# Attention's denominator and numerator in one two-bank PSUM tile, Newton's product in place, and the banks behind it dealt anew

## The chip, the cores and the metric

The kernel runs on one core of a Trainium2 chip. The metric is the device time of one execution in microseconds (us): here the median of three runs of the kernel before, beside one execution that the hardware profiler recorded. Engines are named as the profile names them: PE is TensorE (PEld its weight loads), DVE VectorE, ACT ScalarE, POOL GpSimd, SP SyncE, whose queue issues most DMAs.

## What is computed

Three stages follow one another. The first is a linear attention with random features, over 2 batches of 8 heads, 576 tokens each, head dimension 64 and 128 features. The second is a two-layer network with the activation h·tanh(softplus(h)), the third a mixture of 8 experts that sends each token to the expert with the largest gate logit. The change touches the end of the first, the gate of the third and the places where PSUM is shared out.

```python
def phi(x):                                   # x: q or k, scaled
    h = einsum('bhsd,md->bhsm', x, omega) - sum(x * x, -1) / 2
    return exp(h - max(h, -1)) / sqrt(m)
q_p, k_p = phi(q_s), phi(k_s)
kv  = einsum('bhsm,bhsd->bhmd', k_p, v)
num = einsum('bhsm,bhmd->bhsd', q_p, kv)
den = einsum('bhsm,bhm->bhs', q_p, sum(k_p, axis=2)) + 1e-06
x   = num / den                               # then the network, then:
logits = x @ w_gate; expert = argmax(logits)  # and the two expert matmuls per token
```

## The kernel before

**PSUM.** Every PSUM tile is one bank of 128 partitions by 512 float32 values, handed out by `bank(tag, name)` (L87): three buffers of the tag `pj`, two of `qt`, and one each of `b0`, `b1` and `b2`, eight banks in all. A matmul that writes a tag's only buffer has to wait until every reader of the previous tile of that tag is done.

**Attention** (L169 to L414) works on eight pairs of heads, p = 0 to 7. For each pair POOL, or ACT and DVE for the first ones, splits q and k into a rounded and a residual part (`split`, L213: `kqh`, `kql`); PE projects them on the features, four or five tiles t per pair (`proj`, L222, tile `pj`, three matmuls per product in `mm3`); DVE takes the negated maximum (`phi`, L240, tile `nm`), and DVE and ACT write the exponents (L245, L247, L250, tile `e`). PE turns q's part (`qtr`, L272, tile `qT`) and sums k's with v (`kvm`, L252, tile `kvp` in `b0`). Of the projections, (p, t) = (0, 3) and (1, 3) use `b1`, (1, 0) and (1, 4) use `b2`, all others `pj`.

Two pairs make a **unit** u = 0 to 3. When a unit's sums are complete, `den(u)` (L294) runs in three steps for two token halves c = 0, 1 of 288 tokens (GT) each: eight matmul passes per half into bank `b1` or `b2` (`heads`, L287); on ACT the logarithm and the exponential of its negative, a first estimate r of 1/den (L304, L305); on DVE a Newton step in two instructions, t = (den + eps)·r (L309), then r = (t − 2)·r (L311). Tile t lies in SBUF, so L311 reads two tensors from SBUF, while L309 reads one from PSUM and one from SBUF. `num(u, k)` (L313) runs twice per unit, k = 0 and 1, again with both halves in `b1` and `b2` (in the last unit k = 0 uses the two `qt` banks): eight passes per half on PE, then x = −num·r on DVE (L325), then the split of x into `xh` and `xl`, by POOL in two halves (L59, L63), in the last unit by ACT and DVE over both halves at once.

**Order.** The attention is written as beats (`beat`, L357): in beat t of pair i PE is given the projection (i, t) and whatever `pe` adds, DVE and ACT the work of phi, and the later steps of den and num come one beat after each other. den(u) starts in beat 0 of pair 2u + 3, num(u, 0) in its beat 2, num(u, 1) in beat 0 of pair 2u + 4. The order of instructions on each engine is then fixed when the kernel is built, by a planner that goes by the written order as priority, by estimated costs and by when buffers come free. From L431 on everything is in `manual_schedule`: each engine gets its instructions in the written order.

**Behind it** come the network's first matmul (`hmm`, L157, tile `h`), which starts in the gaps of the last unit, and its second (`ymm`, tile `py`). Column block 0 of `hmm` needs batch 0 alone, block 1 (L549) needs `xh` and `xl` of the last unit. The gate's logits lie in `b0`, `b1` and `b2` (`lg`, L434), are copied out (L800 to L802), turned per group of four token tiles into `b0`, `b1`, `b2` and summed over four parts on DVE, group by group (`route0`, L625, L633). The matmuls `py1` and `py2` of the experts use `b0`, `b1`, `b2` and one `qt` bank for output blocks d = 0 to 3 (L817, L834, L855). The branch from L894 on, for tokens left over, does not run with these inputs.

Of the kernel before, what the change touches and what calls it, by code (L numbers as in the profile page):

```python
# [9 lines left out]
F32 = mybir.dt.float32  # L10
# [5 lines left out]
AF = mybir.ActivationFunctionType  # L16
ALU = mybir.AluOpType
AX = mybir.AxisListType
# [15 lines left out]
def performer_mish_moe(  # L34
# [51 lines left out]

    def bank(tag, name):  # L87
        return psum.tile([128, 512], F32, name=name, tag=tag, bufs={"pj": 3, "qt": 2}.get(tag, 1))


    h3 = tc.alloc_tile_pool(name="h3", bufs=1)
# [77 lines left out]
    with ExitStack() as c2:  # L169
# [8 lines left out]

        wb = a1.tile([128, 512], BF16, name="wb")
        V.memset(wb, 0.0)  # L180
        wp = bank("b2", "wp")
        for _ in range(5):
            T.matmul(out=wp, lhsT=wb[:, 0:128], rhs=wb, start=True, stop=True)
        oms = a1.tile([128, 2 * M], F32, name="oms")
# [37 lines left out]
        def proj(p, t):  # L222
            d = st[p]

            first = {(0, 3): "b1", (1, 0): "b2", (1, 3): "b1", (1, 4): "b2"}
            d["p", t] = ps = bank(first.get((p, t), "pj"), "pj")
            for i in range(2):
                s = slice(256 * t + 128 * i, 256 * t + 128 * i + 128)
                if (p, t) == (0, 0):

                    T.matmul(out=ps[:, i * 256 : i * 256 + 256], lhsT=d["f"][:, s], rhs=oms, start=True, stop=True)
                    continue
                mm3(ps[:, i * 256 : i * 256 + 256], d["h"][:, s], d["l"][:, s], omh, oml, True, True)
# [60 lines left out]
        def den(u):  # L294

            d = st[u, "u"]
            d["r"] = r = a2.tile([128, SEQ], F32, name="r", tag="r", bufs=1)
            o = [bank(f"b{c + 1}", "den")[:, :GT] for c in range(2)]
            half = [r[:, c * GT : c * GT + GT] for c in range(2)]
            for c in range(2):  # L300
                heads(u, o[c], c, "z", slice(0, 32))
            yield
            for c in range(2):
                S.activation(out=half[c], in_=o[c], func=AF.Ln, bias=eps)  # L304
                S.activation(out=half[c], in_=half[c], func=AF.Exp, scale=-1.0)  # L305
            yield
            t = [a2.tile([128, GT], F32, name="t", tag="t") for c in range(2)]
            for c in range(2):
                V.scalar_tensor_tensor(out=t[c], in0=o[c], scalar=EPS, in1=half[c], op0=ALU.add, op1=ALU.mult)  # L309
            for c in range(2):  # L310
                V.scalar_tensor_tensor(out=half[c], in0=t[c], scalar=2.0, in1=half[c], op0=ALU.subtract, op1=ALU.mult)  # L311

        def num(u, k, last=False):  # L313

            b, e = divmod(2 * u, KT)
            r = st[u, "u"]["r"]
            x = a2.tile([128, SEQ], F32, name="xf", tag="xf")
            o = [bank("qt" if last and k == 0 else f"b{c + 1}", "num")[:, :GT] for c in range(2)]
            for c in range(2):
                heads(u, o[c], c, "kv", slice(k * 32, k * 32 + 32))  # L320
            yield
            yield
            for c in range(2):
                s = slice(c * GT, c * GT + GT)
                V.scalar_tensor_tensor(out=x[:, s], in0=o[c], scalar=-1.0, in1=r[:, s], op0=ALU.mult, op1=ALU.mult)  # L325
            c = slice(b * SEQ, b * SEQ + SEQ)
            if last:
                split_hi_lo(x, xh[:, e + k, c], xl[:, e + k, c], "act", "dve")
            else:
                for i in range(2):  # L330
                    s = slice(i * GT, i * GT + GT)
                    t = slice(b * SEQ + i * GT, b * SEQ + i * GT + GT)
                    split_hi_lo(x[:, s], xh[:, e + k, t], xl[:, e + k, t], "pool", "pool")

        eps = a1.tile([128, 1], F32, name="eps")
        V.memset(eps, EPS)
# [94 lines left out]
    with tc.manual_schedule():  # L431
        nc.sync.dma_start(out=wgf, in_=wgate)
        nc.sync.dma_start(out=capi, in_=cap.to_broadcast([TT, 1]))
        lg = [bank(f"b{c}", f"lg{c}")[:, 0:384] for c in range(3)]  # L434

        V.memset(onesb, 1.0)
        V.memset(tiny, 1e-30)
# [187 lines left out]
        def route0(lgs):  # L625
            sh = [TT, NTT, E]
            pv = small("pv", sh)
            for c in range(3):
                p = bank(f"b{c}", "rp")
                for i in range(4):  # L630
                    t = 4 * c + i
                    T.transpose(p[:TT, i * 128 : i * 128 + 128], lgs[:, t * TT : t * TT + TT], ident)
                V.tensor_reduce(  # L633
                    out=pv[:, 4 * c : 4 * c + 4, :],
                    in_=p[:TT, :].rearrange("p (t k e) -> p t e k", k=KT, e=32)[:, :, 0:E, :],
                    op=ALU.add,
                    axis=AX.X,
                )
                yield
            bc = lambda a: a[:, :, None].to_broadcast(sh)  # L640
            mx = small("mx", [TT, NTT])
            V.tensor_reduce(out=mx, in_=pv, op=ALU.max, axis=AX.X)
            V.tensor_tensor(out=pv, in0=pv, in1=bc(mx), op=ALU.subtract)
            ex = small("ex", sh)
            S.activation(out=ex, in_=pv, func=AF.Exp)

            cand = small("cand", sh)
            V.scalar_tensor_tensor(out=cand, in0=pv, scalar=0.0, in1=iota, op0=ALU.is_ge, op1=ALU.mult)
            idx = small("idx", [TT, NTT])
            V.tensor_reduce(out=idx, in_=cand, op=ALU.min, axis=AX.X)  # L650
# [194 lines left out]
        for f in range(8):  # L845
# [9 lines left out]
        py = [bank(t, "py2") for t in ("b0", "b1", "b2", "qt")]  # L855
# [38 lines left out]
    with tc.If(R["nrem"] > 0):  # L894
        with ExitStack() as c2:
# [3 lines left out]
            ob = q1.tile([TT, NTT, DM], F32, name="ob")  # L899
            V.memset(ob, 0.0)  # L900
            with tc.For_i(0, G, 1) as gi:
                ps = [bank(t, "pq") for t in ("pj", "b0", "b1", "b2")]
# [100 lines left out]
```

## Time and profile before

| | |
|---|---|
| three runs, median (lowest to highest) | 314.94 us (311.08 to 315.23) |
| profiled execution: its time, and its span | 315.25 us, span 313.4 us |
| mean granted clock of TensorE | 0.985 of full speed |
| busy share: PE, PEld, DVE, ACT, POOL | 95%, 87%, 67%, 62%, 31% |
| chain that ended last | PE 67%, DVE 16%, ACT 9%, issue 2%, DMA 2%, POOL 1% |

The span runs from the first to the last recorded instruction; the execution's time is 1.85 us longer. The attention fills the first 82 us or so, the network the stretch to about 222 us with the gate near 208 us, the two experts the rest. Busy shares are averages over these stages.

### The profile page before, as it was taken

How to read it: one execution, taken by the hardware profiler on the slowest of the kernel's cores; microseconds unless marked ns; L12 is line 12 of the kernel's file. 1: busy time of each engine (PE TensorE's matmuls, PEld its weight loads, DVE VectorE, ACT ScalarE, POOL GpSimd, SP SyncE). 2: the span in 40 equal slices, each digit the busy share in tenths (PEclk: the TensorE clock that was granted, in tenths of full speed). 3: DMA queues.
4: the chain of work that ended last, by engine and by line, in shares of the span. 5: the costliest groups of instructions: out<-in, count | busy, mean ns of one | idle time of the engine just before them, and what ended most of it. 6: DMA issues, size and time to landing. Idle time of an engine off the chain costs nothing.

```text
span 313.4 us, 6043 instructions
## 1 busy us (share of the span) xinstructions
PE 299.1 (95%) x2276; PEld 272.2 (87%) x2277; DVE 211.0 (67%) x390; ACT 193.9 (62%) x376; POOL 98.1 (31%) x127
## 2 busy tenths in 40 slices
PE   8999979999999999999999989999999999999991
PEld 5897848887899999879987987889899999999991
DVE  4757675894899887988498489999644572325320
ACT  3997754776127897876986997945535743426211
POOL 1889993306012111112010100159304450513300
PEclk9999995999999999999999999999999999999998
DMA  7857611112054727944233000000325535722011
GB/s 228 298 187 262 229 36 51 67 69 69 0 185 153 259 72 232 364 185 153 117 136 134 0 2 0 2 1 3 100 90 152 174 122 163 209 68 78 1 40 44
DMA packets 18066, 37.11 MB, mean 118 GB/s; under 512 B 1552, under 2 KB 7248, under 8 KB 18032
## 3 DMA queue, kind: packets, MB, share of 16 engines
q1 hardware_dynamic: 17888, 36.53, 35.3%
q8 instruction: 20, 0.33, 0.4%
q10 hardware_dynamic: 144, 0.13, 0.2%
q14 instruction: 14, 0.11, 0.1%
HBM read 33.12 MB, written 3.54 MB: 117 GB/s over the span
## 4 chain that ended last, share of the span: by engine, by line
PE 67%; DVE 16%; ACT 9%; issue 2%; DMA 2%; POOL 1%; SPq 0%; DVEq 0%; POOLq 0%; ACTq 0%
PE h L67 7%; PE h L68 6%; PE h L69 6%; PE py L68 5%; PE py L67 5%; PE py L69 5%; PE kvp L259 4%; PE pj L67 3%; PE num L292 3%; DVE g L483 3%; PE pj L69 3%; ACT em L481 3%; PE pj L68 2%; ACT L469 2%; PE qt L280 2%; PE ph L67 2%
## 5 line engine op out<-in xcount | busy, mean ns | idle before, releaser
L67 PE MATMUL h<-xh,wih 128*128 128x384 f32 x192 | 65.7, 342 | 1.6 <-DVE g L440 0.9
L68 PE MATMUL h<-xl,wih 128*128 128x384 f32 x192 | 64.4, 335 | 0.0
L69 PE MATMUL h<-xh,wil 128*128 128x384 f32 x192 | 64.3, 335 | 0.0
L63 POOL TENSOR_TENSOR wl<-wl,whi 128x512 fp32r<-128x512 f32 x27 | 37.3, 1392 | 84.4 <-ACT whi L57 67.2
L67 PEld LDWEIGHTS h<-xh,wih 128*128 128x128 f32 x192 | 36.0, 188 | 5.3 <-issue 3.5
L68 PE MATMUL py<-gh,whi 128*128 128x288 f32 x128 | 38.0, 297 | 0.8 <-DVE gh L63 0.8
L59 POOL TENSOR_SCALAR wih<-wif 128x512 fp32r<-128x512 f32 x13 | 11.7, 899 | 85.0 <-DVE wif L116 60.0
L67 PE MATMUL py<-gh,whi 128*128 128x288 f32 x128 | 38.3, 299 | 0.0
L69 PE MATMUL py<-gh,wl 128*128 128x288 f32 x128 | 37.7, 294 | 0.0
L68 PEld LDWEIGHTS h<-xl,wih 128*128 128x128 f32 x192 | 36.1, 188 | 0.5 <-issue 0.5
L240 DVE TENSOR_REDUCE nm<-pj 128x4 f32<-128x512 f32 x36 | 24.6, 689 | 17.1 <-PE pj L69 17.0
L69 PEld LDWEIGHTS h<-xh,wil 128*128 128x128 f32 x192 | 36.0, 188 | 0.0
L440 ACT COPY g<-h 128x384 f32<-128x384 f32 x36 | 16.0, 472 | 26.7 <-PE h L69 26.5
L63 DVE TENSOR_TENSOR gh<-g,gh 128x288 fp32r<-128x288 f32 x32 | 22.6, 715 | 12.4 <-ACT gh L57 12.3
L247 ACT ACTIVATE e<-pj,nm 128x128 f32<-128x128 f32 x72 | 22.8, 391 | 11.9 <-DVE nm L240 10.8
L483 DVE TENSOR_TENSOR g<-g,em 128x1152 f32<-128x1152 f32 x16 | 21.6, 1357 | 12.7 <-ACT em L481 12.6
L57 ACT CAST whi<-wl 128x512 fp32r<-128x512 f32 x43 | 25.4, 615 | 2.6 <-DMA wl<-w 1.4
L68 PEld LDWEIGHTS py<-gh,whi 128*128 128x128 f32 x128 | 24.1, 188 | 1.5 <-DVE gh L63 1.5
L63 POOL TENSOR_TENSOR kql<-kqf,kqh 128x256 fp32r<-128x256 f32 (+2 forms) x29 | 22.7, 801 | 7.6 <-ACT kqh L57 7.3
L67 PEld LDWEIGHTS py<-gh,whi 128*128 128x128 f32 x128 | 24.0, 188 | 0.9 <-issue 0.6
L69 PEld LDWEIGHTS py<-gh,wl 128*128 128x128 f32 x128 | 24.1, 188 | 0.0
L67 PE MATMUL pj<-omh,kqh 128*128 128x256 f32 x70 | 23.5, 336 | 0.5 <-ACT e L250 0.5
(151 smaller groups left out, 723.9 us busy)
## 6 DMA issues: line engine op xcount, KB each, us to landing
wi<-w_in SPq DMA_DIRECT2D x16, 512.0 KB, 3.6
wo<-w_out SPq DMA_DIRECT2D x16, 512.0 KB, 4.3
wl<-w SPq DMA_DIRECT2D x32, 256.0 KB, 2.8
out<-zero SPq DMA_DIRECT2D x1, 2304.0 KB, 11.9
kqf<-kq SPq DMA_DIRECT2D x3, 640.0 KB, 3.9
v<-va SPq DMA_DIRECT2D x4, 390.0 KB, 4.5
kqf<-kq SPq DMA_DIRECT2D x3, 512.0 KB, 4.0
v<-va SPq DMA_DIRECT2D x4, 260.0 KB, 5.2
```

Source lines behind the costliest of these rows:

```text
L57: S.copy(out=hi, in_=src)
L59: P.tensor_scalar(out=hi, in0=src, scalar1=1.0, scalar2=0.0, op0=ALU.mult, op1=ALU.add)
L63: e.tensor_tensor(out=lo, in0=src, in1=hi.bitcast(F32), op=ALU.subtract)
L67: T.matmul(out=o, lhsT=lh, rhs=rh, start=start, stop=False)
L68: T.matmul(out=o, lhsT=lh, rhs=rl, start=False, stop=False)
L69: T.matmul(out=o, lhsT=ll, rhs=rh, start=False, stop=stop)
L240: d["max"] = V.tensor_reduce(out=nm, in_=pv, op=ALU.max, axis=AX.X, negate=True)
L247: S.activation(out=e[:, j, :], in_=pv[:, j, :], func=AF.Exp, bias=nm[:, j : j + 1])
L259: T.matmul(out=K[:, c : c + 65], lhsT=e[t][:, h, :], rhs=v[:, (2 * t + h) * 65 : (2 * t + h + 1) * 65], start=(p % 2 == 0 and h == 0 and t ...
L292: T.matmul(out=o[32 * i : 32 * i + 32, :GT], lhsT=d[w][:, h, r, s], rhs=d["qT"][:, r, h, c * GT : c * GT + GT], start=True, stop=True, til ...
L440: (S.copy if 2 < j < 14 or (j < 3 and c == 2) else V.tensor_copy)(out=g(j, slice(c * 384, c * 384 + 384)), in_=ps)
L483: V.tensor_tensor(out=hv, in0=hv, in1=em.pop(j), op=ALU.mult)
```

## The change

A new function `twin` allocates one PSUM tile of two banks (tag `b12`), in place of the two tags `b1` and `b2`. den and num use it for both halves: each ACT and DVE step on them becomes one instruction over 2 × 288 values, t is written over den in PSUM, and x is split by POOL in one piece. The last unit's num(3, 0) keeps two `qt` banks and two DVE instructions. Projections (0, 3) and (1, 0) share one twin, (1, 3) and (1, 4) the next. In `route0` all twelve transposes come first, then two sums, one over group 0 and one over groups 1 and 2. The py tiles and the logits take `b0` and the twin's halves through `three`; in the second expert `qt` now holds block 2 and the twin's second half block 3.

```diff
+    def twin(name):
+        return psum.tile([128, 2, 512], F32, name=name, tag="b12", bufs=1)
+    def three(name):
+        t = twin(name)
+        return [bank("b0", name), t[:, 0, :], t[:, 1, :]]
...
-        wp = bank("b2", "wp")
+        wp = twin("wp")[:, 1, :]
...
-            first = {(0, 3): "b1", (1, 0): "b2", (1, 3): "b1", (1, 4): "b2"}
-            d["p", t] = ps = bank(first.get((p, t), "pj"), "pj")
+            if (p, t) in ((0, 3), (1, 3)):
+                st["twin"] = twin("pj")
+            first = {(0, 3): 0, (1, 0): 1, (1, 3): 0, (1, 4): 1}
+            d["p", t] = ps = st["twin"][:, first[p, t], :] if (p, t) in first else bank("pj", "pj")
...
-            d["r"] = r = a2.tile([128, SEQ], F32, name="r", tag="r", bufs=1)
-            o = [bank(f"b{c + 1}", "den")[:, :GT] for c in range(2)]
-            half = [r[:, c * GT : c * GT + GT] for c in range(2)]
+            d["r"] = a2.tile([128, SEQ], F32, name="r", tag="r", bufs=1)
+            r = d["r"].rearrange("p (c t) -> p c t", c=2)
+            o = twin("den")[:, :, :GT]
             for c in range(2):
-                heads(u, o[c], c, "z", slice(0, 32))
+                heads(u, o[:, c, :], c, "z", slice(0, 32))
             yield
-            for c in range(2):
-                S.activation(out=half[c], in_=o[c], func=AF.Ln, bias=eps)
-                S.activation(out=half[c], in_=half[c], func=AF.Exp, scale=-1.0)
+            S.activation(out=r, in_=o, func=AF.Ln, bias=eps)
+            S.activation(out=r, in_=r, func=AF.Exp, scale=-1.0)
             yield
-            t = [a2.tile([128, GT], F32, name="t", tag="t") for c in range(2)]
-            for c in range(2):
-                V.scalar_tensor_tensor(out=t[c], in0=o[c], scalar=EPS, in1=half[c], op0=ALU.add, op1=ALU.mult)
-            for c in range(2):
-                V.scalar_tensor_tensor(out=half[c], in0=t[c], scalar=2.0, in1=half[c], op0=ALU.subtract, op1=ALU.mult)
+            V.scalar_tensor_tensor(out=o, in0=o, scalar=EPS, in1=r, op0=ALU.add, op1=ALU.mult)
+            V.scalar_tensor_tensor(out=r, in0=o, scalar=2.0, in1=r, op0=ALU.subtract, op1=ALU.mult)
...
-            o = [bank("qt" if last and k == 0 else f"b{c + 1}", "num")[:, :GT] for c in range(2)]
+            if last and k == 0:
+                o = [bank("qt", "num")[:, :GT] for c in range(2)]
+            else:
+                t = twin("num")[:, :, :GT]
+                o = [t[:, c, :] for c in range(2)]
...
-            for c in range(2):
-                s = slice(c * GT, c * GT + GT)
-                V.scalar_tensor_tensor(out=x[:, s], in0=o[c], scalar=-1.0, in1=r[:, s], op0=ALU.mult, op1=ALU.mult)
+            if last and k == 0:
+                for c in range(2):
+                    V.scalar_tensor_tensor(out=x3[:, c, :], in0=o[c], scalar=-1.0, in1=r[:, c, :], op0=ALU.mult, op1=ALU.mult)
+            else:
+                V.scalar_tensor_tensor(out=x3, in0=t, scalar=-1.0, in1=r, op0=ALU.mult, op1=ALU.mult)
...
-            if last:
-                split_hi_lo(x, xh[:, e + k, c], xl[:, e + k, c], "act", "dve")
-            else:
-                for i in range(2):
...
-                    split_hi_lo(x[:, s], xh[:, e + k, t], xl[:, e + k, t], "pool", "pool")
+            split_hi_lo(x, xh[:, e + k, c], xl[:, e + k, c], *(("act", "dve") if last else ("pool", "pool")))
...
-        lg = [bank(f"b{c}", f"lg{c}")[:, 0:384] for c in range(3)]
+        lg = [x[:, 0:384] for x in three("lg")]
...
-            for c in range(3):
-                p = bank(f"b{c}", "rp")
+            r0, r12 = bank("b0", "rp"), twin("rp")
+            for c, p in enumerate((r0, r12[:, 0, :], r12[:, 1, :])):
                 for i in range(4):
...
-                V.tensor_reduce(
...
-                yield
+            for o, p in ((pv[:, 0:4, :], r0[:TT, :]), (pv[:, 4:12, :], r12[:TT, :, :].rearrange("p c f -> p (c f)"))):
+                V.tensor_reduce(out=o, in_=p.rearrange("p (t k e) -> p t e k", k=KT, e=32)[:, :, 0:E, :], op=ALU.add, axis=AX.X)
+            yield
...
-        ps1 = [bank(t, "py1") for t in ("b0", "b1", "b2", "qt")]
+        ps1 = [*three("py1"), bank("qt", "py1")]
...
-        py = [bank(t, "py2") for t in ("b0", "b1", "b2", "qt")]
+        py = three("py2")
+        py.insert(2, bank("qt", "py2"))
```

## Rows read from the trace of the kernel before

**Rows 1.** the page, busy time, share and instructions of TensorE and its weight loads

```profile
PE 299.1 (95%) x2276; PEld 272.2 (87%) x2277; DVE 211.0 (67%) x390; ACT 193.9 (62%) x376; POOL 98.1 (31%) x127
```

**Rows 2.** the chain that ended last, 40 to 56 us (start, us, what)

```profile
43.15 3.40 DVE r L311
46.55 0.38 DVE t L309
...
47.06 0.69 PE num L292 x8
```

**Rows 3.** who waited for whom (total us, times, longest)

```profile
PE num L292 <- DVE t L309: 2.1, 1, 2.1
```

**Rows 4.** by stretch: length; PE, PEld, DVE, ACT, POOL busy; PEclk; DMA share; GB/s

```profile
44.90:47.06 2.16, 0.03 (x1) 0.03 (x1) 2.16 (x3) 0.00 (x0) 2.08 (x4) 1.00 0.00 0
47.06:54.60 7.54, 7.54 (x43) 6.37 (x47) 4.04 (x9) 3.52 (x12) 2.53 (x5) 0.55 0.19 53
```

**Rows 5.** timeline of DVE, 20 to 50 us (start, us, engine, line, operation)

```profile
26.20 0.89 DVE L311 SCALAR_TENSOR_TENSOR r<-t,r 128x288 f32<-128x288 f32 x1
...
43.07 3.48 DVE L311 SCALAR_TENSOR_TENSOR r<-t,r 128x288 f32<-128x288 f32 x1
```

**Rows 6.** timeline of POOL, 18 to 50 us

```profile
44.45 1.42 POOL L63 TENSOR_TENSOR kql<-kqf,kqh 128x256 fp32r<-128x256 f32 x2
45.84 0.41 POOL L59 TENSOR_SCALAR kqh<-kqf 128x256 fp32r<-128x256 f32 x1
46.33 0.81 POOL L63 TENSOR_TENSOR kql<-kqf,kqh 128x256 fp32r<-128x256 f32 x1
```

**Rows 7.** DVE groups by line and shape (count, busy us, mean ns)

```profile
L311 DVE SCALAR_TENSOR_TENSOR r<-t,r 128x288 f32<-128x288 f32 x8 | 7.3, 920 | 0.0
...
L325 DVE SCALAR_TENSOR_TENSOR xf<-num,r 128x288 f32<-128x288 f32 x16 | 6.8, 451 | 1.1 <-PE num L292 1.0
...
L63 DVE TENSOR_TENSOR xl<-xf,xh 128x576 fp32r<-128x576 f32 x2 | 1.5, 760 | 0.0
```

**Rows 8.** ACT group of 576 elements, by line and shape

```profile
L57 ACT CAST xh<-xf 128x576 fp32r<-128x576 f32 x2 | 1.4, 678 | 2.1 <-DVE xf L325 2.1
```

**Rows 9.** timeline of all engines, 60 to 82 us (unit 2)

```profile
65.76 0.82 DVE L311 SCALAR_TENSOR_TENSOR r<-t,r 128x288 f32<-128x288 f32 x2
...
66.60 1.18 PE L292 MATMUL num<-qT,kv 128*32 128x288 f32 x16
...
70.11 0.43 POOL L59 TENSOR_SCALAR xh<-xf 128x288 fp32r<-128x288 f32 x1 [11.69 <-DVE xf L325]
```

**Rows 10.** the chain that ended last, 20 to 34 us (unit 0)

```profile
23.81 0.62 PE den L292 x8
...
26.90 0.62 PE num L292 x8
...
28.75 0.62 PE num L292 x8
...
31.93 1.11 PE num L292 x16
33.04 0.32 PE pj L67
```

**Rows 11.** timeline of all engines, 0 to 20 us

```profile
12.89 0.36 PE L67 MATMUL pj<-omh,kqh 128*128 128x256 f32 x1
...
13.03 0.62 ACT L250 ACTIVATE e<-pj,nm 128x128 f32<-128x128 f32 x2
```

**Rows 12.** timeline of all engines, 76.5 to 92 us (unit 3)

```profile
78.86 1.18 PE L292 MATMUL num<-qT,kv 128*32 128x288 f32 x16
...
81.11 1.49 DVE L63 TENSOR_TENSOR xl<-xf,xh 128x576 fp32r<-128x576 f32 x2
...
84.24 0.33 PE L67 MATMUL h<-xh,wih 128*128 128x384 f32 x1
```

**Rows 13.** timeline of all engines, 200 to 226 us

```profile
208.48 0.81 DVE L633 TENSOR_REDUCE pv<-rp 96x32 f32<-96x128 f32 x3
```

More of the change, by code (lines that the diff above doesn't have):

```diff
@@ L296, in den @@
             d = st[u, "u"]
-            d["r"] = r = a2.tile([128, SEQ], F32, name="r", tag="r", bufs=1)
-            o = [bank(f"b{c + 1}", "den")[:, :GT] for c in range(2)]
-            half = [r[:, c * GT : c * GT + GT] for c in range(2)]
+            d["r"] = a2.tile([128, SEQ], F32, name="r", tag="r", bufs=1)
+            r = d["r"].rearrange("p (c t) -> p c t", c=2)
+            o = twin("den")[:, :, :GT]
             for c in range(2):
-                heads(u, o[c], c, "z", slice(0, 32))
+                heads(u, o[:, c, :], c, "z", slice(0, 32))
             yield
-            for c in range(2):
-                S.activation(out=half[c], in_=o[c], func=AF.Ln, bias=eps)
-                S.activation(out=half[c], in_=half[c], func=AF.Exp, scale=-1.0)
+            S.activation(out=r, in_=o, func=AF.Ln, bias=eps)
+            S.activation(out=r, in_=r, func=AF.Exp, scale=-1.0)
             yield
-            t = [a2.tile([128, GT], F32, name="t", tag="t") for c in range(2)]
-            for c in range(2):
-                V.scalar_tensor_tensor(out=t[c], in0=o[c], scalar=EPS, in1=half[c], op0=ALU.add, op1=ALU.mult)
-            for c in range(2):
-                V.scalar_tensor_tensor(out=half[c], in0=t[c], scalar=2.0, in1=half[c], op0=ALU.subtract, op1=ALU.mult)
+            V.scalar_tensor_tensor(out=o, in0=o, scalar=EPS, in1=r, op0=ALU.add, op1=ALU.mult)
+            V.scalar_tensor_tensor(out=r, in0=o, scalar=2.0, in1=r, op0=ALU.subtract, op1=ALU.mult)
         def num(u, k, last=False):
             b, e = divmod(2 * u, KT)
-            r = st[u, "u"]["r"]
+            r = st[u, "u"]["r"].rearrange("p (c t) -> p c t", c=2)
             x = a2.tile([128, SEQ], F32, name="xf", tag="xf")
-            o = [bank("qt" if last and k == 0 else f"b{c + 1}", "num")[:, :GT] for c in range(2)]
+            x3 = x.rearrange("p (c t) -> p c t", c=2)
+            if last and k == 0:
[3 more added lines that the diff above has]
+                o = [t[:, c, :] for c in range(2)]
             for c in range(2):
@@ L322, in num @@
             yield
-            for c in range(2):
-                s = slice(c * GT, c * GT + GT)
-                V.scalar_tensor_tensor(out=x[:, s], in0=o[c], scalar=-1.0, in1=r[:, s], op0=ALU.mult, op1=ALU.mult)
-            c = slice(b * SEQ, b * SEQ + SEQ)
-            if last:
-                split_hi_lo(x, xh[:, e + k, c], xl[:, e + k, c], "act", "dve")
-            else:
-                for i in range(2):
-                    s = slice(i * GT, i * GT + GT)
-                    t = slice(b * SEQ + i * GT, b * SEQ + i * GT + GT)
-                    split_hi_lo(x[:, s], xh[:, e + k, t], xl[:, e + k, t], "pool", "pool")
+            if last and k == 0:
[3 more added lines that the diff above has]
+                V.scalar_tensor_tensor(out=x3, in0=t, scalar=-1.0, in1=r, op0=ALU.mult, op1=ALU.mult)
+            c = slice(b * SEQ, b * SEQ + SEQ)
+            split_hi_lo(x, xh[:, e + k, c], xl[:, e + k, c], *(("act", "dve") if last else ("pool", "pool")))
         eps = a1.tile([128, 1], F32, name="eps")
@@ L632, in route0 @@
                     T.transpose(p[:TT, i * 128 : i * 128 + 128], lgs[:, t * TT : t * TT + TT], ident)
-                V.tensor_reduce(
[L634 to L638, printed above, removed]
-                yield
+            for o, p in ((pv[:, 0:4, :], r0[:TT, :]), (pv[:, 4:12, :], r12[:TT, :, :].rearrange("p c f -> p (c f)"))):
+                V.tensor_reduce(out=o, in_=p.rearrange("p (t k e) -> p t e k", k=KT, e=32)[:, :, 0:E, :], op=ALU.add, axis=AX.X)
+            yield
             bc = lambda a: a[:, :, None].to_broadcast(sh)
@@ L833, in performer_mish_moe @@
                     expert_load(R["eB"], 1, c)
-        py = [bank(t, "py2") for t in ("b0", "b1", "b2", "qt")]
+        py = [*three("py2"), bank("qt", "py2")]
         for f in range(8):
@@ L854, in performer_mish_moe @@
                 nc.sync.dma_start(out=rows(0, slice(0, DM)), in_=o)
-        py = [bank(t, "py2") for t in ("b0", "b1", "b2", "qt")]
+        py = three("py2")
+        py.insert(2, bank("qt", "py2"))
         yo = h3.tile([128, KT, GT], F32, name="yo", tag="em2")
@@ L901, in performer_mish_moe @@
             with tc.For_i(0, G, 1) as gi:
-                ps = [bank(t, "pq") for t in ("pj", "b0", "b1", "b2")]
+                ps = [bank("pj", "pq"), *three("pq")]
                 for j in range(NJ):
```

## The prediction

> **What bounds the kernel now.** The page comes first: PE is busy for 95% of the span [rows 1], so work taken off DVE, ACT or POOL is worth something only where PE waits for it, and the question is where PE loses time in the part that the change touches. The chain that ended last answers it. Between 40 and 56 us it runs along PE's matmuls, leaves them for one DVE instruction of 3.40 us, and comes back to PE with a num group at 47.06 [rows 2]. The list of waits gives the same place as PE's longest wait for another engine in the attention: num waited 2.1 us, once, for L309 [rows 3]. The table by stretch shows the price. From 44.90 to 47.06 us PE worked for 0.03 us; in the 7.54 us that follow it is busy all the time, but at a granted clock of 0.55 [rows 4], which is nearly all at the lower of its two levels, 1.2 GHz in place of 2.4. So the reader sees one event with two bills: an idle gap, and a slow stretch behind it.
>
> The cause is in DVE's timeline. L311 of unit 1, first half, took 3.48 us, against 0.89 us for the same instruction in unit 0 [rows 5]; L309 of the second half stood behind it in DVE's queue, and PE's num for that half needs the bank that L309 reads. POOL meanwhile ran its splits without a gap: 44.45 + 1.42 meets 45.84, that one ends at 46.25, the next starts at 46.33, and L311 ends just behind this first gap, at 46.55 [rows 6]. By shape, the 16 L325, which read one operand from PSUM and one from SBUF, average 451 ns on the same 288 columns, while the eight L311, both operands in SBUF, average 920 [rows 7]. Where POOL sits idle (11.69 us before 70.11), two L311 take 0.82 us together, back to back [rows 9]. I read this as DVE held off SBUF, on its second operand, as long as POOL keeps coming.
>
> One page of the Trainium skill puts the price elsewhere. "SBUF — State Buffer", section "SBUF: two separate sides", says that a VectorE instruction with two SBUF inputs and a GpSimd instruction that reads SBUF exclude each other, that whichever starts first holds the port pair for its instruction, and that the other is blocked. Read literally, the wait ends with the POOL instruction under way; no row here agrees, for L311 outlasted several. That reading is the second rival below.
>
> **The change part by part.** The sum is made on the profiled execution, 315.25 us, whose span is 313.4; it lies 0.31 above the median of the runs shown (314.94).
>
> *The Newton step.* Its second instruction now reads t from PSUM and r from SBUF, the form of L325. Four instructions of 576 columns replace eight L311, and four replace eight L309. For one of 576 columns the nearest row is xl, 760 ns [rows 7]; two of 451 in a row would be 902; I take 0.76. The writing of t into PSUM has no row; its nearest is again L325, which reads PSUM, so 0.76 to 0.90. If the reading above is right, the 3.48 us become one 0.76, and the 2.1 us wait goes [rows 3]: **−2.1**. With the gap goes what followed it: 7.54 us at 0.55 is work for 7.54 × 0.55 = 4.15 us at full clock, **−3.4** [rows 4]. PE had work all through that stretch, so nothing else is late at once. If the clock falls anyway these 3.4 stay, which is kept for the range.
>
> *Fewer, longer num groups.* In unit 0 PE does num(0, 0) in two groups, at 26.90 and at 28.75, each of 0.62 us with a first projection matmul behind it that is exposed, because its weights load late (0.32 us, as at 33.04); num(0, 1) is one group of 1.11 us [rows 10]. Two groups cost 2 × (0.62 + 0.32) = 1.88; one costs 1.11 + 0.32, and one ordinary projection matmul more, which I put at half the exposed one or less, 0.15: 1.58. Since the twin comes free as a whole, the groups of units 0 and 1 should merge: 2 × 0.3 = **−0.6** (0 to −0.9; den's halves may stay apart).
>
> *Added wait: num(u, 0) behind the whole Newton step.* Before, a bank was free once L309 had read it. Now t stays in it, so both halves wait until L311's successor is done. In unit 0 den's last matmul ends at 23.81 + 0.62 = 24.43 [rows 10]; then come two ACT passes of 576 columns (0.68 each, as the cast of xh [rows 8]) and two of DVE (0.76 each): 24.43 + 2.88 = 27.31 at the earliest. Before, the halves started at 26.90 and 28.75. An order that keeps the first place would wait 0.4 us, or up to 1.85 if other ACT and DVE work comes between; behind the waiting matmul stand all later projections, turns and kv sums, for PE runs them in order. In unit 2 the pair of L311 ended at 66.58 and num started at 66.60 [rows 9]: no change beyond 0.3. But the order is planned anew with the new costs, and in unit 0 it had already put the second half late enough. So 0 to 4 us over three units; I take a small one, **+0.4**, nearest to the 27.31 against 26.90.
>
> *The first pairs.* Projection (1, 3) needs the twin of (0, 3) and (1, 0), and so also the last exponent of (1, 0). PE started (1, 3) at 12.89; that exponent ended at 13.03 + 0.62 = 13.65 [rows 11]. The bounds are 0 (other work fills it) and 0.8; I take **+0.3**.
>
> *The tail.* num(3, 1) started at 78.86, right after L309 of the second half. It now waits for both Newton instructions, some 1.0 us longer; the matmuls `h` of the network can fill that, since they need only earlier units. Block 1 of the network starts at 84.24, and xl is complete at 81.11 + 1.49 = 82.60 [rows 12]: 1.6 us of cover. **+0.2**, bounds 0 and 1.1; if that cover is gone, each further microsecond counts in full.
>
> *Work that hides.* The split of x in one piece keeps POOL longer in one instruction, but nothing reads these columns before the network, and in unit 2 POOL stood idle for 11.69 us [rows 9]; the last split of q and k ended at 47.14 [rows 6]. ACT's merged steps save time in an engine that PE does not wait for here. In the gate, three sums took 0.81 us from start to end [rows 13]; two do the same columns with one start fewer, but begin later: −0.2 to +0.2, taken as 0. Logits, py1 and py2 get banks whose readers are done a whole matmul phase earlier; block 3 of the second expert alternates as before: 0. No DMA is added or moved past a queue.
>
> Sum: −2.1 − 3.4 − 0.6 + 0.4 + 0.3 + 0.2 = −5.2, so 315.25 − 5.2 = **310.0 us**. The lowest run shown, 311.08, would fit an execution in which L311 was held up for less, without most of the slow stretch; I can't see that in one trace.
>
> **The rivals.**
> 1. *The stall goes, new waits take half of it back.* num(u, 0) keeps its place in the order and waits in units 0 and 1 by about 1.3 us each, without a fall of the clock: 310.0 + 2.6 = 312.6. For it: 27.31 is already later than 26.90. Against it: unit 0's second half stood at 28.75 without a wait.
> 2. *L311's length is not POOL's doing, or only one instruction of it.* Then the change takes one POOL instruction, about 0.74 (half of 1.42 rounded up by its overlap) [rows 6], and the rest of the stall and the slow stretch stay: 314.5. Against it: the end of L311 behind POOL's first gap, and 0.82 for two with POOL idle.
> 3. *Slower.* The whole-tile release makes PE wait for 2.1 us or more, in one place after another, as the gap of [rows 4] did, and each such wait brings its own slow stretch. One costs 2.1 + 3.4 = 5.5 and gives 315.5, no change; it decides from the second on: 310.0 + 11.0 = 321.0. For it: the two ACT and two DVE passes are now in series over both halves. Against it: the worst wait found above is 1.85 us, and PE's order is planned for the new costs.
> 4. *More than the forecast.* den's halves merge as well (three units, 0.3 each), the added waits vanish: 315.25 − 5.5 − 0.6 − 0.9 = 308.2, and a little lower in a luckier execution.
>
> **How the numbers follow.** The forecast has 0.60 (about 308.6 to 311.8), the first rival 0.15, the second 0.06, the third 0.07, the fourth 0.12. Two per cent, about what a measurement of this kernel can tell from no change, is 6.3 us: faster by more means below 308.6, slower above 321.2. Faster: the fourth rival and the edge of the forecast, 0.12 + 0.10 = 0.22. Slower: part of the third, 0.05. Within 2%: 0.73. The range reaches down to the fourth rival with an unlucky bound taken off, 307.3, and up past the first and the lower edge of the second, 313.9; outside are the third, most of the second and a tail, 2 in 10.
>
> **What would show it.** Right: no DVE instruction over 1 us in the attention, the two Newton instructions near 0.76 us whatever POOL does; no wait of PE on DVE of 2 us; granted clock 1.00 from 20 to 80 us; the network's block 1 starting near 79 us instead of 84.24. The first rival shows as waits of num on the Newton step; the third as the same with a clock below 1 behind it; the second as a Newton instruction that is still long while POOL is busy. The forecast is wrong if the clock is 1.00 throughout and the time is still above 313, for then PE was not what bounded the stretch.

## The result, and the profile after

The changed kernel takes 310.25 us (median of 19 runs, 309.37 to 310.72), the kernel before in the same comparison 313.18 (19 runs, 311.07 to 315.62): a ratio of 0.992, 95% interval 0.990 to 0.994. The profiled execution of the changed kernel took 309.82 us, its span is 308.0. Between the two profiled executions lie 5.4 us, between the two medians 2.9; why these differ is one of the findings below.

The page's first part, which answers to [rows 1], shows PE's busy time 3.4 us lower with the same 2276 instructions, and its share higher:

```profile
PE 295.7 (96%) x2276; PEld 269.5 (88%) x2277; DVE 206.2 (67%) x374; ACT 193.1 (63%) x368; POOL 95.6 (31%) x115
```

By stretch, where [rows 4] had the gap and the clock of 0.55 (start and end; length; busy time of PE, PEld, DVE, ACT, POOL; PEclk; DMA share; GB/s): PE is busy throughout, at full clock.

```profile
40.00:50.00 10.00, 10.00 (x101) 8.27 (x97) 7.26 (x13) 7.18 (x22) 7.20 (x13) 1.00 0.14 42
50.00:60.00 10.00, 10.00 (x92) 8.78 (x92) 9.17 (x16) 8.04 (x23) 2.88 (x3) 1.00 0.25 67
```

DVE's groups of the attention, which answer to [rows 5, 7] (count, busy us, mean ns, idle before): four Newton instructions of each kind, 759 and 749 ns whatever POOL does, as the 0.76 taken for them.

```profile
L338 DVE SCALAR_TENSOR_TENSOR xf<-num,r 128x576 f32<-128x576 f32 x7 | 5.3, 754 | 4.1 <-PE num L302 1.8 <-POOL xl L63 1.4 <-issue 1.0
...
L316 DVE SCALAR_TENSOR_TENSOR den<-den,r 128x576 f32<-128x576 f32 x4 | 3.0, 759 | 3.2 <-ACT r L314 3.2
L317 DVE SCALAR_TENSOR_TENSOR r<-den,r 128x576 f32<-128x576 f32 x4 | 3.0, 749 | 0.0
```

The chain, where [rows 10] had den and num in two groups of eight: x16 is one group of both halves. In unit 0 den and both nums are whole; in unit 1 den stays in two groups, both nums are whole.

```profile
23.07 1.16 PE den L302 x16
...
29.62 1.11 PE num L302 x16
...
31.85 1.11 PE num L302 x16
...
38.45 0.62 PE den L302 x8
...
39.51 0.62 PE den L302 x8
...
46.16 1.11 PE num L302 x16
```

The list of PE's waits, where [rows 3] had num waiting 2.1 us, no longer has num. What it has in its place lies behind the attention: before, the first of these lines read 0.8 in total, 0.6 the longest, and the second 0.3.

```profile
PE py L68 <- DVE gh L63: 1.6, 2, 1.0
...
PE ph L67 <- DVE h L761: 0.9, 1, 0.9
```

So something was won and something given back. The same instruction in both timelines tells how much. The last of the network's four early copies out of `h` starts at 87.98 us before and at 81.46 after, 6.5 us earlier. The gate's first turned logits (`rp`) come at 207.49 and 200.92, 6.6 earlier; the `py` matmul behind the gate that waits for `gh` at 212.49 and 206.91, only 5.6; the first expert's first `ph` at 252.17 and 246.77, 5.4; the `ph` that waits for `h` at 257.43 and 252.60, 4.8; PE's last matmuls (`pt`) at 306.57 and 301.75, 4.8. Of the 6.5 us, 1.7 are given back: 1.0 at the gate, 0.6 in the first expert, 0.1 between. The end of the span is 5.4 us earlier all the same (313.4 and 308.0), because what lies behind PE's last matmul, where the last output leaves by DMA, took 6.2 us before and 5.6 after. In the nine profiles of kernels without an added block (below) this last stretch takes 5.6 to 6.2 us, whatever the edit, so these 0.6 us are put down to chance.

The rows of the give-back, before (the idle time in brackets is the engine's, with what ended it):

```profile
205.89 0.48 ACT L802 COPY lgs<-lg 128x384 f32<-128x384 f32 x1 [0.81 <-PE lg L489]
206.49 0.54 DVE L801 COPY lgs<-lg 128x384 f32<-128x384 f32 x1
...
212.49 0.40 PE L68 MATMUL py<-gh,whi 128*128 128x288 f32 x1 [0.19 <-DVE gh L63]
...
253.19 1.30 ACT L615 CAST yt<-py 128x288 fp32r<-128x288 f32 x4
...
257.43 0.40 PE L67 MATMUL ph<-yt,whi 128*128 128x288 f32 x1 [0.33 <-DVE h L758]
```

and in the changed kernel:

```profile
198.06 0.48 ACT L803 COPY lgs<-lg 128x384 f32<-128x384 f32 x1 [0.83 <-PE lg L496]
199.95 0.54 DVE L804 COPY lgs<-lg 128x384 f32<-128x384 f32 x1
200.53 0.48 ACT L805 COPY lgs<-lg 128x384 f32<-128x384 f32 x1 [1.99 <-DVE lgs L804]
...
206.91 0.40 PE L68 MATMUL py<-gh,whi 128*128 128x288 f32 x1 [1.01 <-DVE gh L63]
...
250.93 0.70 ACT L622 CAST yt<-py 128x288 fp32r<-128x288 f32 x2 [2.62 <-DVE yt L623]
...
252.60 0.40 PE L67 MATMUL ph<-yt,whi 128*128 128x288 f32 x1 [0.87 <-DVE h L761]
```

L804 and L805 read different banks, but these are two halves of one tile, and the ACT copy starts only when the DVE copy is done. Before, that ACT copy ran ahead of the DVE copy, after 0.81 us of waiting for PE alone. The casts and subtractions of `yt` show the same: before, four casts ran in one stretch of 1.30 us; now the third waits 2.62 us for a DVE subtraction on the other half of its twin.

How long ACT has to wait there is again a matter of DVE beside POOL. Ahead of the DVE copy stand two subtractions of `gh` (2.98 us for both at 197.05; one alone takes 0.46), ahead of the subtractions of `yt` two of `wl` (3.46 us for both at 246.70; one alone takes 0.69). All four read two tensors from SBUF while POOL works on `wl`. They are as slow before (2.98 at 203.59, 3.47 at 252.08), but there ACT did not wait for them.

### The profile page after: what moved, and what is told of

The parts are those of the page before. It is cut to its first block, busy times and chain, and to the rows that moved or that the text cites. A ratio compares the mean times of both kernels' runs of the same rounds, so it can differ in the third digit from the quotient of the medians.

```text
span 308.0 us, 6011 instructions
## 1 busy us (share of the span) xinstructions
PE 295.7 (96%) x2276; PEld 269.5 (88%) x2277; DVE 206.2 (67%) x374; ACT 193.1 (63%) x368; POOL 95.6 (31%) x115
## 4 chain that ended last, share of the span: by engine, by line
PE 69%; DVE 15%; ACT 10%; issue 2%; POOL 1%; DMA 1%; DVEq 0%; POOLq 0%; ACTq 0%
PE h L67 7%; PE h L69 6%; PE h L68 6%; PE py L68 6%; PE py L69 6%; PE py L67 6%; PE kvp L269 4%; PE pj L67 3%; DVE gh L63 3%; PE pj L69 3%; PE num L302 3%; PE pj L68 3%; DVE g L490 3%; ACT em L488 3%; PE qt L290 2%; ACT L476 2%
## 5 line engine op out<-in xcount | busy, mean ns | idle before, releaser
L63 DVE TENSOR_TENSOR wl<-wl,whi 128x512 fp32r<-128x512 f32 x21 | 16.5, 787 | 8.6 <-POOL wl L63 4.3
```

The source lines that it names most:

```text
L63: e.tensor_tensor(out=lo, in0=src, in1=hi.bitcast(F32), op=ALU.subtract)
```

## The experiments

**The Newton product in place, nothing else.** The kernel before with t written over den in its own bank; the two tags `b1` and `b2` stay, den and num keep their groups.

```diff
-            t = [a2.tile([128, GT], F32, name="t", tag="t") for c in range(2)]
...
-                V.scalar_tensor_tensor(out=t[c], in0=o[c], scalar=EPS, in1=half[c], ...)
+                V.scalar_tensor_tensor(out=o[c], in0=o[c], scalar=EPS, in1=half[c], ...)
...
-                V.scalar_tensor_tensor(out=half[c], in0=t[c], scalar=2.0, in1=half[c], ...)
+                V.scalar_tensor_tensor(out=half[c], in0=o[c], scalar=2.0, in1=half[c], ...)
```

> The kernel before with one edit: Newton's product t is written over den in its own bank, so the second Newton instruction reads one operand from PSUM. Banks b1 and b2 and the two halves stay. If the length of that instruction is POOL's doing, through its second SBUF operand, none of the eight now takes over 0.6 us, PE has no wait of 2 us on DVE in the attention, the granted clock is 1.00 from 20 to 75 us, and the time is 309.5 to 311.0 us with a spread of the runs under 2 us, as narrow as the changed kernel's 309.4 to 310.7. If it was the order of the merged program that removed the stall, an instruction of over 1 us stays, and the time is that of the kernel before, 313.2 us with a spread of some 4 us.

309.37 us (6 runs), ratio 0.988 (0.985 to 0.991), just below the range expected; the runs spread over 1.2 us. The group of the second instruction, against 920 ns in [rows 7]:

```profile
L310 DVE SCALAR_TENSOR_TENSOR r<-den,r 128x288 f32<-128x288 f32 x8 | 3.5, 449 | 0.0
```

PE has no wait for DVE at num and the clock is 1.00 from 10 to 80 us. The whole gain of the change comes without the twin; the two intervals overlap, so no more than that is claimed. The plan of all engines moved a little with this edit, so it doesn't show by itself that POOL was the cause.

**The other half: merged, but t in SBUF.** The changed kernel with a 576-wide t in SBUF again.

```diff
-            V.scalar_tensor_tensor(out=o, in0=o, scalar=EPS, in1=r, op0=ALU.add, op1=ALU.mult)
-            V.scalar_tensor_tensor(out=r, in0=o, scalar=2.0, in1=r, op0=ALU.subtract, op1=ALU.mult)
+            t = a2.tile([128, 2, GT], F32, name="t", tag="t")
+            V.scalar_tensor_tensor(out=t, in0=o, scalar=EPS, in1=r, op0=ALU.add, op1=ALU.mult)
+            V.scalar_tensor_tensor(out=r, in0=t, scalar=2.0, in1=r, op0=ALU.subtract, op1=ALU.mult)
```

> The changed kernel with one edit: t lies in an SBUF tile of 2 x 288 columns, so the second Newton instruction of 576 columns again reads two operands from SBUF; the twin comes free one instruction earlier. If the two SBUF operands are the cause, that instruction is again longer than 0.75 us where POOL runs without a gap (units 0 and 1, 1 to 4 us) and 0.75 us where POOL is idle, and the time is 311 to 315 us with a spread of 2 us or more, the more the longer PE is left without work. If merging the halves is what helped, all four take 0.75 us and the time is 310.2 us or less, as the bank comes free earlier.

310.44 us (6 runs), ratio 0.990 (0.987 to 0.993): as the changed kernel. The expectation missed, in its length as in its time; its rival (0.75 us four times) came in units 2 and 3 alone, with 0.97 in unit 0. The timelines of DVE and of POOL in unit 1:

```profile
45.37 1.02 DVE L318 SCALAR_TENSOR_TENSOR r<-t,r 128x576 f32<-128x576 f32 x1
```

```profile
44.33 1.45 POOL L63 TENSOR_TENSOR kql<-kqf,kqh 128x256 fp32r<-128x256 f32 x2
45.72 0.94 POOL L59 TENSOR_SCALAR kqh<-kqf 128x256 fp32r<-128x256 f32 x1
```

Both operands lie in SBUF and POOL is busy, yet the instruction loses only 0.27 us (1.02 against 0.75 to 0.76 with POOL idle): it got in where POOL went from its residuals to the next rounded part, and that POOL instruction took 0.94 in place of 0.41. Two operands in SBUF are therefore not enough for a long hold-up. Merging also moved the instruction in POOL's row; that this is what spared it is not shown.

**The kernel before, once more.** Word for word, for the spread of its time.

> The kernel before, word for word, for a second profile and the granted clock of each of its runs. If its spread (311.07 to 315.62 us) comes from how long POOL holds off the second Newton instruction, this profile has another sum of time in its eight instructions of that kind than the first one's 7.3 us, and over the runs the time falls as the granted clock rises: near 0.985 at 315 us, 0.995 at 311 us. If the spread comes from elsewhere, time and clock of the runs are unrelated.

313.22 us (12 runs), ratio 0.998 (0.995 to 1.001); its profiled execution took 312.21. The Newton instruction of unit 1 is long again (num waited 2.4 us for L309), but the clock stayed:

```profile
42.90 3.79 DVE L311 SCALAR_TENSOR_TENSOR r<-t,r 128x288 f32<-128x288 f32 x1
```

```profile
40.00:50.00 10.00, 7.56 (x70) 5.72 (x70) 8.18 (x11) 5.44 (x17) 8.63 (x16) 1.00 0.05 19
50.00:60.00 10.00, 10.00 (x96) 8.58 (x94) 8.00 (x16) 7.73 (x27) 3.88 (x6) 1.00 0.31 94
```

The first profile has 0.89 and 0.77 in these two stretches. All eight L311 take 7.1 us here and 7.3 in the first profile [rows 7], so the spread isn't theirs. The hold-up is there both times, and the fall of the clock behind it is not: the gate's `rp` starts at 204.48 us here and at 207.49 there. Over the 29 executions of this kernel in the comparison the time goes with the clock, as expected: the three fastest (311.49 to 311.93 us) have a mean granted clock of 0.994 to 0.997, the four above 315 us 0.982 to 0.984. The lowest times lie about 1 us below 312.21, which had no fall of the clock; what makes up that rest is open, since no execution as fast was profiled.

**The twin kept, its halves dealt so that no reader waits for the other engine's.** The changed kernel with three edits; each of the first two was also run alone.

```diff
         lg = [x[:, 0:384] for x in three("lg")]
+        lg = [lg[1], lg[0], lg[2]]
...
             for d in range(KT):
                 S.copy(out=yt[:, 0, d, :], in_=ps[d][:, :GT])
+            for d in range(KT):
                 V.tensor_tensor(out=yt...)
...
         py = [*three("py2"), bank("qt", "py2")]
+        py = [py[1], py[0], py[2], py[3]]
```

> The changed kernel with the two halves of a twin given to one engine each time: the logits' middle block goes to b0, so that ACT copies both halves and DVE the other bank; in yfin all four casts on ACT come before the four subtractions on DVE; the first expert's blocks 0 and 2 (both copied by DVE) take the twin. The theory: readers of a twin's halves on different engines are put one behind the other, and that gave back 1.0 us at the gate (PE waits for gh) and 0.5 us at the first expert (PE waits for h). Then the waits of ACT on the DVE copy (2.0 us), of ACT's cast on DVE's subtraction (2.6 us) and of DVE's copy on ACT's (0.8 us) go, PE's wait for gh falls from 1.0 us to 0.2 and that for h from 0.9 to 0.3, and the time is 308.7 to 309.3 us against 310.25. If the give-back is only the later stages' own drift, the waits go and the time stays 310.0 to 310.5.

All three: 308.85 us (6 runs), ratio 0.986 (0.983 to 0.989), an interval apart from the changed kernel's. The two edits alone, in a later comparison (before 313.23):

> The changed kernel with one edit: the gate's logits take b0 for the middle block of columns and the twin's halves for the first and the last, so that the DVE copy out of one half is no longer held behind the ACT copy out of the other for long. The theory (of the 6.5 us won in the attention 1.1 to 1.6 are given back where two engines read the two halves of one twin in turn; the gate has one such place, with 2.0 us of wait on DVE's copies and about 0.8 us more wait of py for gh): 309.4 to 309.9 us against 310.3 of the change, py's wait for gh back from 1.0 to 0.4 or less. The rival (the gate has nothing to do with it, the give-back sits in the first expert alone): 310.3, as the change.

> The changed kernel with the other edit alone: in the step that turns the network's output block into two halves, all four casts on ACT are written ahead of the four subtractions on DVE, so that a cast of one half of a twin isn't ordered behind the subtraction on the other half. The theory: the casts run in one stretch again (four in about 1.3 us, none waiting 2.6 us on DVE), ph's wait for the first of them goes from 0.9 to 0.3 us, and the time is 309.4 to 309.9 us. The rival (the gate alone gives back): 310.3, as the change.

The gate's alone gives 309.71 (6 runs, ratio 0.988, 0.985 to 0.991), the casts' alone 309.94 (6 runs, ratio 0.989, 0.986 to 0.992, just above what was expected). Each interval overlaps the changed kernel's; the traces tell the two apart. With the gate's edit py waits 0.39 us where it waited 1.01, and ph still 0.9; with the casts' edit, whose list of PE's waits follows, py's wait stands and ph's is 0.3 again.

```profile
PE py L68 <- DVE gh L63: 1.7, 2, 1.0
...
PE ph L67 <- DVE h L762: 0.3, 1, 0.3
```

From the first `rp` to the py that waits, 5.00 us pass before, 5.99 in the changed kernel, 5.21 with the gate's edit, 5.99 with the casts' and 5.19 with all three. So the gate's edit takes back 0.8 us of the 1.0 lost there, and the casts' edit the 0.6 of ph's wait. With all three nothing is given back behind it: the early copy out of `h` (81.87) is 6.1 us earlier than before and PE's last matmuls (300.55) are 6.0. The third edit was not run alone.

**POOL's order alone.** The kernel before; PE, DVE and ACT issue the same instructions in the same order, t stays in SBUF. Only POOL (and with it a few DMA issues on SP) is reordered.

```diff
-        e.tensor_tensor(out=lo, in0=src, in1=hi.bitcast(F32), op=ALU.subtract)
+        return e.tensor_tensor(out=lo, in0=src, in1=hi.bitcast(F32), op=ALU.subtract)
...
-                split_hi_lo(d["f"][:, c], d["h"][:, c], d["l"][:, c], *e)
+                with tc.issue_after(st["lo"].ins) if "lo" in st and e[0] == "pool" else ExitStack(): st["lo"] = split_hi_lo(d["f"][:, c], d["h"][:, c], d["l"][:, c], *e)
```

> The kernel before with POOL's order alone changed: each split of q and k is issued as residual behind its own rounded part, one pair after another, where before two rounded parts came first and then two residuals. PE, DVE and ACT keep their order, the Newton step keeps both operands in SBUF. A residual that reads what the instruction just before it wrote starts 0.08 to 0.09 us late (the 0.41 that ended at 46.25 and the one that began at 46.33 in the profile of before), while two of a kind in a row leave no gap. Theory A (an SBUF-only DVE instruction gets in at POOL's first gap, however many instructions that is away): every pair now has a gap, no Newton instruction takes over 1.3 us, num's wait of 2.1 to 2.6 us for the first instruction of the other half is gone, and the time falls to 308.5 to 311 us, like the kernel with t in PSUM. Theory B (chance, or something else at this place): the 3.5 to 3.9 us stay, and the time with them, 311 to 315.

309.26 us (4 runs), ratio 0.988 (0.982 to 0.995). The timelines of DVE and POOL in unit 1, against [rows 5, 6]:

```profile
42.34 0.97 DVE L311 SCALAR_TENSOR_TENSOR r<-t,r 128x288 f32<-128x288 f32 x1
```

```profile
42.25 0.75 POOL L63 TENSOR_TENSOR kql<-kqf,kqh 128x256 fp32r<-128x256 f32 x1
42.95 0.63 POOL L59 TENSOR_SCALAR kqh<-kqf 128x256 fp32r<-128x256 f32 x1
43.66 0.74 POOL L63 TENSOR_TENSOR kql<-kqf,kqh 128x256 fp32r<-128x256 f32 x1
```

L311 starts beside a residual and gets in when it ends, though POOL leaves no gap there (42.25 + 0.75 meets 42.95); the rounded part behind it takes 0.63 in place of 0.41. So theory A's time came, but not by its mechanism. PE is busy 10.00 of 10 us in every stretch from 20 to 80 us, at clock 1.00, and num waits for nothing. This is the cleanest result of the study: L311 keeps its operands, its place and its neighbours, POOL alone is changed, and the stall is gone. That POOL's order caused the stall is shown by it; by which rule the order does so is not.

**The disputed cost by itself.** Three kernels with a block of POOL and DVE work behind the end of the kernel before; its inputs and outputs are scratch tiles, and each row of POOL work runs beside DVE instructions of 288 columns, one operand in PSUM and both in SBUF in turn. The second and third have POOL's two orders, without gaps and in pairs; the third lets DVE's instructions overlap. The edit shown is the second's.

```diff
+            for k in range(3):
...
+                    if k == 0:
+                        hi(i)
+                        hi(i + 1)
+                        lo(i)
+                        lo(i + 1)
+                    else:
+                        hi(n % 4)
+                        lo(n % 4)
...
+                    V.scalar_tensor_tensor(out=dc, in0=dp, scalar=1.0, in1=da, op0=ALU.add, op1=ALU.mult)
+                    V.scalar_tensor_tensor(out=dc, in0=da, scalar=2.0, in1=db, op0=ALU.subtract, op1=ALU.mult)
```

> The kernel before with a block of work behind its end that computes nothing of the result: POOL issues 20 subtractions of 128x256 in a row, then 26 multiply-adds of one operand, then 24 of both kinds in turn, then one alone; beside each, DVE issues in turn five instructions of 288 columns with one operand in PSUM and five with both in SBUF. The time is longer by the block and says nothing; the DVE instructions of the block are read from the trace. Theory A (an SBUF-only DVE instruction is held off as long as POOL has work, to POOL's first gap): the first SBUF-only instruction beside each POOL row lasts to the end of that row, 8 to 14 us, and the PSUM ones 0.45. Theory B (it is held to the end of the POOL instruction under way): 0.6 to 1.2 us beside subtractions, 0.5 to 0.9 beside multiply-adds, none over 1.5. Theory C (it gets in by chance, at some change of POOL's instruction): a spread from 0.5 to several us within one row. With POOL idle all theories expect 0.41 to 0.45.

> The kernel before with a block of work behind its end that computes nothing of the result: POOL issues first 24 instructions of 128x256 as two rounded parts and two residuals in turn (no gap between them, as in the attention), then 24 as pairs, each residual behind its own rounded part (a gap of 0.08 us in each), and then nothing; beside each row DVE issues in turn five instructions of 288 columns with one operand in PSUM and five with both in SBUF. The time says nothing. Theory A (held to POOL's first gap): in the first row an SBUF-only instruction lasts several us, up to the row's end, some 14 us; in the second none over 1.4 us. Theory B (held to the end of the POOL instruction under way): none over 1.2 us in either row. The PSUM ones 0.46 in all rows by both.

> The kernel before with the same block behind its end as in the run before (POOL without gaps, then in pairs with gaps, then idle), but on DVE each instruction has a tile of its own and the SBUF-only one writes over its own second operand, as the Newton step does, so that it starts while the instruction before it is still under way (L311 in the attention began 0.08 us before the end of the one ahead of it, while in the block before every instruction began 0.03 us behind it). If that overlap is what lets POOL keep DVE out: SBUF-only instructions of 2 us and more in the first row, at most 1.3 in the second, 0.45 in the third. If not: none over 1.2 in any row, and what holds L311 for 3.5 to 4.1 us in the attention stays open beyond POOL's order. The time says nothing; the embedded attention gives one more profile of L311 and of the stretch behind its gap.

In no row did an SBUF-only instruction take over 0.97 us, so theory A of the second kernel's expectation and the overlap of the third both missed. The first kernel doesn't test theory A: all its POOL instructions write one tile, and behind each one stands a gap of 0.08 us. In the first kernel they took 0.46 beside subtractions, 0.53 beside multiply-adds and 0.46 to 0.75 beside both; with POOL idle 0.46. Its theory B missed beside subtractions: DVE lost nothing there and POOL paid, with 0.90 us a subtraction in place of 0.61. The PSUM ones took 0.44 to 0.46 throughout. From the timelines of the second kernel, without gaps on POOL:

```profile
306.30 0.94 DVE L926 SCALAR_TENSOR_TENSOR dc<-da,db 128x288 f32<-128x288 f32 x1
...
307.77 0.46 DVE L926 SCALAR_TENSOR_TENSOR dc<-da,db 128x288 f32<-128x288 f32 x1
```

```profile
305.52 1.41 POOL L908 TENSOR_TENSOR ml<-ma,mh 128x256 fp32r<-128x256 f32 x2
306.89 0.98 POOL L905 TENSOR_SCALAR mh<-ma 128x256 fp32r<-128x256 f32 x2
```

The DVE instruction waits for the residual under way, 0.48 us, and then POOL is the one held: its two rounded parts take 0.98 in place of 0.77. No gap was needed. Overlapping DVE's instructions made no difference (0.97 and less). "Held to POOL's first gap" is thus wrong as a rule. It fits L311 of unit 1, first half, in every profile of the attention of before, those of the three blocks among them:

| profile | long L311, us | num's wait, us | clock 40 to 50, 50 to 60 us |
|---|---|---|---|
| before | 3.48 | 2.1 | 0.89, 0.77 |
| before, once more | 3.79 | 2.4 | 1.00, 1.00 |
| first block | 3.92 | 2.6 | 0.84, 0.82 |
| second block | 4.07 | 2.7 | 1.00, 1.00 |
| third block | 3.77 | 2.4 | 0.91, 0.92 |

In each of the five L311 ends 0.30 or 0.31 us behind the rounded part after which POOL leaves a gap, as 46.55 behind 46.25 in [rows 2, 6]. But it does not fit unit 0 of the same executions, where the two L311 take 0.45 to 0.98 us with POOL as busy. The second one of the first profile, and POOL's two rounded parts beside it:

```profile
29.07 0.74 DVE L311 SCALAR_TENSOR_TENSOR r<-t,r 128x288 f32<-128x288 f32 x1
```

```profile
29.11 0.97 POOL L59 TENSOR_SCALAR kqh<-kqf 128x256 fp32r<-128x256 f32 x2
30.05 1.44 POOL L63 TENSOR_TENSOR kql<-kqf,kqh 128x256 fp32r<-128x256 f32 x2
```

It let one rounded part pass (29.11 to 29.50) and got in before the next, where POOL left no gap.

## Why the prediction was right, and where not

**What bounds the kernel: right.** The gap and the stretch behind it were where PE lost time, and L311 beside POOL was their cause. The in-place kernel removes both without the twin, and POOL's order alone does too, with L311 as it was.

**"DVE held off SBUF as long as POOL keeps coming": right for this place, too wide as a rule.** POOL does hold it, over six or seven POOL instructions (the one under way at its start among them) in five of five profiles. But beside a row without gaps in the blocks, in the merged kernel with t in SBUF and in unit 0 of the same kernel it got in at the first or second change of POOL's instruction. What decides between the two stays open. The second rival's literal reading, that the wait ends with the POOL instruction under way, describes the blocks and not unit 1 of the attention. The prediction's "no row here agrees" was too strong: the L311 at 26.20 in [rows 5] took 0.89, which is one such wait. As a forecast of the time, 314.5, that rival fell. The Trainium skill, "SBUF — State Buffer", "SBUF: two separate sides", says that the engine that starts first keeps the shared pair for that instruction and the other is blocked; the blocks agree with it (0.94 against 0.46), the 3.48 us do not.

**−2.1 for the wait: right. −0.6 for the num groups: the groups merged, the price isn't shown.** The wait is gone; num(0) of units 0 and 1 is one group each. den of unit 0 merged as well, which the forecast left to its fourth rival. The early copy out of `h` starts at 81.46 us in the changed kernel, at 81.87 in the dealt one, but at 82.32 with the product in place and at 81.90 with POOL in pairs, which keep PE's groups of eight: merging is worth 0.9 us at most by these, and by the last pair nothing.

**−3.4 for the slow stretch: right for the execution it was made on, mis-sized for the median.** The gates of the two profiles of before are 207.49 − 204.48 = 3.0 us apart, and the second shows no fall of the clock. By the table of five profiles two lost nothing to the clock, one lost 1.7 us, (0.09 + 0.08) × 10, and two lost 3.4. The prediction put the lowest run, 311.08, down to two things, a shorter hold-up of L311 and less of the slow stretch. The times that go with the clock bear out the second. The profiles speak against the first, for the hold-up was longer in the execution of 312.21 us than in the one of 315.25.

**+0.4, +0.3 and +0.2 for added waits: too high.** PE is busy 10.00 of 10 us in every stretch from 10 to 80 us. num came later in the order (29.62 us in unit 0), with projections and kv sums ahead of it, so the whole-tile release cost nothing. Without these 0.9 us the sum is −6.1, near the 6.5 that the attention gained, and the first rival (312.6) and the third (321.0) did not come.

**"Logits, py1 and py2 get banks whose readers are done a whole matmul phase earlier ... 0": wrong, and the step that failed.** It looked at when a bank comes free for the next writer, and not at two engines that read the two halves of one tile. These readers are put in order, with waits of 1.99 and 2.62 us on ACT, and PE paid for them at py (1.0 us) and ph (0.6). The gate's sums took 0.61 us where three took 0.81, but they end 2.8 us behind the first `rp` where they ended 1.8 behind it, outside the ±0.2; with the gate's edit it is 2.0, so most of that delay was the readers' order too.

**The total: close by luck.** The attention gained 6.5 us where 5.2 were forecast, then 1.7 were given back where 0 stood, and 0.6 came from the last stretch by chance: 5.4 between the profiled executions. So 5.2 is closer than the steps deserve. Between the medians the change is worth 2.9 us, because the median of before has less of the slow stretch than the execution that the sum was made on.

**The signs.** No wait of PE on DVE of 2 us, a clock of 1.00 from 20 to 80 us and Newton instructions near 0.76 came. The network's block 1 starts at 77.72 us, before the 79 that was named. "No DVE instruction over 1 us" failed: L122 took 1.32 at 49.72 and L120 1.03 at 53.86, work on weights beside POOL's split of x, for which PE did not wait.

The best of the kernels run are the dealt twin (308.85), POOL in pairs (309.26) and the product in place (309.37); their intervals overlap, so no order among them is claimed. All three have medians below both kernels'; only the dealt twin's interval is clear of the changed kernel's.

## What to carry to other kernels

When one instruction on an engine is several times as long as others of its kind, look at what the neighbouring engine issues beside it, and try that engine's order before rebuilding buffers: here a reorder of POOL was worth as much as the whole change. When two banks become one tile, list every pair of readers on different engines, since here they waited for each other. And price a slow clock behind a gap from more than one profile: the gap may be in all of them, the clock's fall in some.

## What was not expected

The hold-up is not one instruction long and not the same everywhere: 3.48 to 4.07 us in all at one place in five of five profiles, 0.45 to 0.98 for the same line in unit 0, at most 0.97 for the same shapes in blocks of their own. Where DVE gets in, POOL pays (0.94 in place of 0.41, 0.98 in place of 0.77). And a gap of 2.1 to 2.7 us on PE was followed by a granted clock of 0.55 in one profile and of 1.00 in two others, the longest gap among them.
